# HGRN2 attention and a max-out FFN in one kernel: the first part reordered, and the block loads issued in odd units

## The chip, the cores and the metric

The kernel runs on one core of one Trainium2 chip. The metric is the device time of that core in microseconds (us). Three runs of the kernel before took 503.63, 503.81 and 504.72 us; their median is 503.81. Engines have their short names: PE is TensorE (matrix products), PEld its weight loads, DVE is VectorE, ACT is ScalarE, POOL is GpSimd, SP is the sync engine, whose queue issues most of the DMAs. "SPq" and "ACTq" in the profile are the issuing queues of SP and ACT.

## What is computed

Attention first, with B = 4 batches, H = 8 heads, S = 768 steps and D = 48; then an FFN over the 3072 tokens with model width 384 and hidden width 768. All is fp32.

```
f = 1 / (1 + exp(-f_logit))
for t in range(S):
    state = f[:, :, t, :, None] * state + einsum('bhd,bhe->bhde', k[:, :, t], v[:, :, t])
    y[:, :, t] = einsum('bhd,bhde->bhe', q[:, :, t], state)
x = y.transpose(0, 2, 1, 3).reshape(B * S, H * D)
h = maximum(maximum(x @ w1, x @ w2), x @ w3)
out = h @ w_out
```

The FFN weights arrive as 64-bit words and are rounded to fp32 on the chip.

## The kernel before, in words

**Units and groups.** The work of the attention is cut into 24 units (NU). Unit u is a chunk of 64 time steps (c = u // 2) of a pair of batches (u % 2), so 128 tokens. Four units (GRP) are one group of 512 tokens, and each of the six groups gets one FFN.

**Functions of a unit.** `load` (L161) fetches f, k and q: for units below 8 by rows, two DMAs a tensor (L158); from unit 8 on by blocks, for two units at once, as 24 DMAs (L173), called where u is even. `load_v` (L178) fetches v with two DMAs. `sigmoids` makes the gates, `after` a backward scan (L273) and kh (L280), `before` a forward scan (L287) and qh (L291), `carry` (L297) the decayed state, `keys` (L306) transposes kh and copies it to ks on ACT (L308), `pairs` (L319, L322) makes the masked products at, `values` (L333, L342) the outputs y and the new state (st, L350), `finish` (L363) adds what comes from the state and copies y to `heads` on ACT (three copies, L369). `pack` (L373) rearranges heads into xT, the FFN's input, by ten DMAs (L380). It is called as pack(0, 2) for three units of a group, on SP, and as pack(3, 3) for the last, five DMAs on SP and five on ACT in turn. In the first group it is one call for all four units, on both queues.

**FFN.** `ffn` (L385) is a generator. Its 18 steps are three products 128x512 each (L392; a product shows as two records of the profile), with the maximum kept on ACT (L396) and DVE (L398), into hm. Its four out groups are six products 128x384 each (L411), a copy to `o` on ACT (L414) and two DMAs to the output (L418). `fill(n)` (L423) runs n such pieces of the FFN at a place of the attention's code; so each engine's order is written out by hand in the schedule (L437 to L535), and the FFN of a group runs between the units of the next.

**Buffers.** The pool `work` has two buffers a name (o, top, xT), unless a number is given; hm has one. Of the PSUM tiles named p for the FFN there are two. The copy of out group i + 2 thus waits for the two output DMAs of group i, and the product after next waits for that copy.

**Weights.** There are 24 pieces: 18 of w1 to w3 and 6 of w_out. `load_weights` (L190) fetches raw words (L199), at most 12 pieces ahead. `round_begin` (L203) has two ACT instructions (L211, L216), two on DVE (L212, L213) and an add on POOL (L217); `round_end` (L220) one on DVE (L225) that writes w_in or w_out. Three pieces are rounded in the first part, the others inside ffn(0), one ahead. `pad_blocks` (L140) writes constants beside the block loads with six POOL memsets, after units 4 and 6.

**Queues.** The DMAs of SP are issued in the order of the code. In the built program each DMA issue of SP and ACT takes one of eight completion semaphores, which the two queues share, and an issue waits until the DMA before it on the same semaphore has landed.

**End.** After the last FFN, DVE, TensorE and DVE again (L538 to L543) compute `low`, which says whether a gate product fell below a limit; SP, TensorE and the others read it (L732) and branch (L733) to a general version, which does not run with these inputs.

The loop around the places that the change touches is this:

```
for u in range(GRP, NU):
    n = u + 1
    fill(2 if u % 2 and u > 2 * GRP else 1)
    keys(u)
    if u > GRP:
        finish(u - 1)
        if u % GRP == 3:
            pack(0, 2, xT)
        elif u % GRP == 0:
            pack(3, 3, xT, both)
```

Of the kernel before, what the change touches and what calls it, by code (L numbers as in the profile page):

```python
# [9 lines left out]
FP32 = mybir.dt.float32  # L10
I32 = mybir.dt.int32
U32 = mybir.dt.uint32
AF = mybir.ActivationFunctionType
ALU = mybir.AluOpType
# [40 lines left out]
def kernel(  # L55
# [32 lines left out]
    def fast():  # L88
        ctx = ExitStack()
        with ctx:  # L90
# [47 lines left out]
                    nc.vector.memset(t[:, :, D:DP], pad)  # L138

            def pad_blocks(i):  # L140
                for nm, pad in PADS.items():
                    for p0 in (32, 96):
                        nc.gpsimd.memset(blocks[nm][i][p0:p0 + 32, :, :, D - 32:], pad)

            NLD = 4
            BY_ROWS = 8
# [31 lines left out]
            def load_v(u):  # L178
                load_tokens(v_tiles[u % NLD], v, u)
# [20 lines left out]

            halfway = {}

            def round_begin(n):  # L203
                if n in raw:
                    words = raw[n].rearrange("p (c two) -> p c two", two=2)
                    lo, hi = words[:, :, 0], words[:, :, 1]

                    top = work.tile([128, PIECE], U32, name="top_bits", bufs=4)  # L210
                    nc.scalar.activation(top.bitcast(FP32), hi.bitcast(FP32), AF.Abs)  # L211
                    nc.vector.tensor_scalar(top.bitcast(FP32), top.bitcast(FP32), HI_MIN, None, op0=ALU.max)  # L212
                    nc.vector.tensor_scalar(top, top, 3, 0x3FFFFFF8, op0=ALU.logical_shift_left, op1=ALU.bitwise_and)  # L213

                    rest = work.tile([128, PIECE], U32, name="rest_bits", bufs=3)
                    nc.scalar.activation(rest, lo, AF.Copy, scale=2.0 ** -29)  # L216
                    nc.gpsimd.tensor_tensor(top, top, rest, op=ALU.add)  # L217
                    halfway[n] = (top, hi)

            def round_end(n):  # L220
                if n in raw:
                    top, hi = halfway.pop(n)
                    dst = pieces[n][0].bitcast(U32)
                    by = lambda t: t.rearrange("p (a c) -> p a c", a=dst.shape[1])
                    nc.vector.scalar_tensor_tensor(dst, by(hi), 0xC0000000, by(top),  # L225
                                                   op0=ALU.bitwise_and, op1=ALU.bitwise_or)
                    raw.pop(n)
# [157 lines left out]
            def ffn(g, xT):  # L385
                hm = work.tile([128, NJ, TOK], FP32, name="hm", bufs=1)
                for j in range(NJ):
                    top = None
                    for i in range(3):
                        p = ps_f.tile([128, TOK], FP32, name="p")  # L390
                        for kt in range(NK):
                            nc.tensor.matmul(p, lhsT=w_in[i][:, kt, j * 128:(j + 1) * 128], rhs=xT[:, kt, :],  # L392
                                             start=(kt == 0), stop=(kt == NK - 1))
                        if i == 0:
                            top = work.tile([128, TOK], FP32, name="top")
                            nc.scalar.copy(top, p)  # L396
                        else:
                            nc.vector.tensor_tensor(hm[:, j, :] if i == 2 else top, p, top, op=ALU.max)  # L398

                        if g == 0:  # L400
                            step, last = 3 * j + i, 3 * NJ
                            for r in range(*(3 + (len(pieces) - 3) * n // last for n in (step, step + 1))):
                                round_end(r)
                                if r + 1 < len(pieces):
                                    round_begin(r + 1)
                            load_weights(2, r + 1)
                        yield
                for i in range(GRP):
                    p = ps_f.tile([128, TOK], FP32, name="p")
                    for j in range(NJ):  # L410
                        nc.tensor.matmul(p[:, 0:DM], lhsT=hm[:, j, i * UT:(i + 1) * UT], rhs=w_out[:, j, :],  # L411
                                         start=(j == 0), stop=(j == NJ - 1))
                    o = work.tile([UT, DM], FP32, name="o")
                    nc.scalar.copy(o, p[:, 0:DM])  # L414
                    c, bp = divmod(g * GRP + i, 2)
                    for a in range(2):
                        t0 = (2 * bp + a) * S + c * C
                        nc.sync.dma_start(out=out[t0:t0 + C, :], in_=o[a * C:(a + 1) * C, :])  # L418
                    yield
# [3 lines left out]
            def fill(n):  # L423
                while n and pending:
                    try:
                        next(pending[0])
                        n -= 1
                    except StopIteration:
                        pending.pop(0)

            def new_xT():
                return work.tile([128, NK, TOK], FP32, name="xT")

# [3 lines left out]
            with tc.manual_schedule():  # L437
# [2 lines left out]
                load(1, one, "kq")  # L440
                load_v(0)
                load(2)
                load_v(1)
                load(3)
                load_weights(3)
                load_v(2)
                load_v(3)
                xT = new_xT()
                sigmoids(0)
# [8 lines left out]
                for u in range(2):  # L458
                    values(u)
                    keys(u + 1)  # L460
                    after(u + 2)
                    carry(u + 2)
                    pairs(u + 1)
                    finish(u)
                    before(u + 2)
                    if u == 0:
                        sigmoids(3)
                values(2)
                keys(3)
                finish(2)  # L470
                load_weights(3)
                load(GRP)
                load_v(GRP)
                round_begin(0)
                pairs(3)
                round_begin(1)
                round_begin(2)
                values(3)
                for n in range(3):
                    round_end(n)  # L480
                round_begin(3)

                nc.tensor.transpose(ps_tr.tile([128, 128], FP32, name="tr"), ident, ident)
                finish(3)
                pack(0, GRP - 1, xT, both)
                load_weights(3)
                load(GRP + 1)
                load_v(GRP + 1)
# [7 lines left out]
                fill(1)  # L496
                for u in range(GRP, NU):
                    n = u + 1
                    fill(2 if u % 2 and u > 2 * GRP else 1)
                    keys(u)  # L500
                    if u > GRP:
                        finish(u - 1)
# [4 lines that stand above are left out]
                    if u % GRP == 0:  # L507
                        if u > GRP:
                            pending.append(ffn(u // GRP - 1, xT))
                        xT = new_xT()  # L510
                    pairs(u)
                    if u + 2 < NU and (u % 2 == 0 or u + 2 < BY_ROWS):
                        load(u + 2)
                    if u + 2 < NU:
                        load_v(u + 2)
                    if n < NU:
                        sigmoids(n)
                    fill(1)
                    if n < NU:
                        after(n)  # L520
                    fill(1)
                    values(u)
                    if n < NU:
                        before(n)
                        carry(n)
                        if n in (5, 7):
                            pad_blocks(n // 2 % 2)
                    fill(1)
                    if u >= 2 * GRP:
                        fill(1)  # L530
                fill(1)
                finish(NU - 1)
                pack(3, 3, xT, both)
                pending.append(ffn(NU // GRP - 1, xT))
                fill(99)  # L535


            least = work.tile([128, 1], FP32, name="least")  # L538
            nc.vector.tensor_reduce(out=least, in_=ends.rearrange("p u a -> p (u a)"), op=ALU.min, axis=AX.X)
            nc.vector.tensor_scalar(least, least, P_MIN, None, op0=ALU.is_lt)  # L540
            n_low = ps_tr.tile([1, 1], FP32, name="tr")
            nc.tensor.matmul(n_low, lhsT=least, rhs=ones, start=True, stop=True)
            nc.vector.tensor_copy(low, n_low)  # L543

    def general():
        G, AHEAD = 128, 3
# [218 lines left out]
```

## Time and profile before

| | us |
|---|---|
| median of three runs | 503.81 |
| the profiled execution | 504.31 |
| its span in the trace | 502.6 |
| PE busy | 467.9 (93%) |
| DVE busy | 217.2 (43%) |
| ACT busy | 108.7 (22%) |
| POOL busy | 98.7 (20%) |
| L392 (FFN products), busy | 291.9 |
| L411 (out products), busy | 98.8 |

The mean granted TensorE clock is 0.966. The page cuts the span in 40 equal slices; a digit is the busy share of a slice in tenths, and 9 is 90% or more. The chain is the work that ended last, followed back from the last instruction to what released it. A row of a group gives the line, the engine, the tiles out<-in, the shape and the count, then the busy time, the mean ns of one instruction, and the idle time of the engine just before them with what ended most of it. A line of the waits gives the engine and line that waited, what it waited for, the us in total, the times and the longest. A line of the timeline gives the start and length in us, the engine and line, and in brackets the idle time ahead of it with its releaser.

### The profile page before, as it was taken

The numbers are of one execution on the slowest core, as the hardware profiler recorded it, in microseconds if no ns is written. First come the engines' busy times: TensorE is split into PE (matmuls) and PEld (weight loads), VectorE is DVE, ScalarE is ACT, GpSimd is POOL, SyncE is SP. The second block draws the span as 40 slices with busy tenths as digits, with TensorE's granted clock in tenths as the row PEclk, the third lists the DMA queues.
The fourth block names the chain that finished last, engine by engine and source line by source line (L and its number), as shares of the span: only waits on it lengthen the run. The fifth ranks groups of instructions, "written<-read, shape, count | busy, mean of one in ns | idle before, by whom it ended". The sixth has DMA issues, their size and how long they took to land.

```text
span 502.6 us, 9969 instructions
## 1 busy us (share of the span) xinstructions
PE 467.9 (93%) x4067; PEld 250.9 (50%) x4067; DVE 217.2 (43%) x346; ACT 108.7 (22%) x227; POOL 98.7 (20%) x132
## 2 busy tenths in 40 slices
PE   5755999996989999999999999999999999999994
PEld 4642555543635455645545654545644545544452
DVE  7852787787225435135535226533325620012100
ACT  2340445540212211202220211220220111100000
POOL 2111356564021212021112022112112200000000
PEclk9875999998999999999999999999999999999998
DMA  9995996720156612266602276402460011200011
GB/s 129 199 179 157 268 243 143 93 59 1 40 87 109 88 27 65 46 79 110 85 2 63 56 88 109 66 16 57 78 105 18 1 36 37 55 0 0 1 28 42
DMA packets 170007, 38.51 MB, mean 77 GB/s; under 512 B 154976, under 2 KB 168800, under 8 KB 169952
## 3 DMA queue, kind: packets, MB, share of 16 engines
q1 hardware_dynamic: 166208, 36.50, 41.5%
q10 hardware_dynamic: 3744, 1.28, 1.3%
q8 instruction: 34, 0.56, 0.5%
q14 instruction: 21, 0.17, 0.1%
HBM read 28.31 MB, written 4.72 MB: 66 GB/s over the span
## 4 chain that ended last, share of the span: by engine, by line
PE 80%; DVE 6%; DMA 4%; SPq 4%; ACT 1%; issue 1%; POOL 1%; ACTq 0%; DVEq 0%; POOLq 0%
PE p L392 53%; PE p L411 17%; SPq L158 3%; PE y L363 2%; PE y L333 2%; DMA xT<-heads 2%; PE a L319 2%; PE tr L306 2%; PE y L342 1%; DMA v_ld<-in_v_dram 1%; POOL top_bits L217 1%; PE tr L234 1%; DVE top_bits L213 1%; DMA k_ld<-in_k_dram 1%; DVE top_bits L212 1%
## 5 line engine op out<-in xcount | busy, mean ns | idle before, releaser
L392 PE MATMUL p<-xT,w_in 128*128 128x512 f32 x648 | 291.9, 602 | 7.3 <-DMA xT<-heads 5.1
L392 PEld LDWEIGHTS p<-xT,w_in 128*128 128x128 f32 x648 | 120.5, 191 | 147.0 <-issue 134.1
L411 PE MATMUL p<-w_out,hm 128*128 128x384 f32 x288 | 98.8, 501 | 4.3 <-DVE w_out L225 4.3
L411 PEld LDWEIGHTS p<-w_out,hm 128*128 128x128 f32 x288 | 55.5, 195 | 44.7 <-DVE w_out L225 5.6
L398 DVE TENSOR_TENSOR top<-p,top 128x512 f32<-128x512 f32 x36 | 24.8, 690 | 106.3 <-PE p L392 106.3
L396 ACT COPY top<-p 128x512 f32<-128x512 f32 x36 | 21.1, 586 | 191.5 <-PE p L392 191.5
L279 POOL COPY ends<-r 128x8 f32<-128x8 f32 x24 | 4.6, 193 | 194.2 <-DVE r L273 194.2
L398 DVE TENSOR_TENSOR hm<-p,top 128x512 f32<-128x512 f32 x36 | 24.6, 684 | 38.2 <-PE p L392 38.2
L322 DVE TENSOR_TENSOR at<-a,mask 128x512 f32<-128x512 f32 x24 | 16.5, 689 | 52.8 <-PE a L319 52.8
L217 POOL TENSOR_TENSOR top_bits<-top_bits,rest_bits 128x384 uint32<-128x384 uint32 x24 | 27.2, 1133 | 50.3 <-DVE top_bits L213 27.9
L414 ACT COPY o<-p 128x384 f32<-128x384 f32 x24 | 11.4, 477 | 107.8 <-PE p L411 99.0
L287 DVE TENSOR_TENSOR_SCAN prod<-gate,from_inv 128x520 f32<-128x520 f32 x24 | 32.4, 1349 | 0.0
L273 DVE TENSOR_TENSOR_SCAN r<-gate,from_one 128x520 f32<-128x520 f32 x24 | 30.9, 1288 | 2.9 <-issue 2.2
L369 ACT COPY heads<-y 64x256 f32<-64x256 f32 (+1 forms) x72 | 26.6, 369 | 14.3 <-PE y L363 13.3
L291 POOL TENSOR_TENSOR qh<-qt,prod 128x512 f32<-128x512 f32 x16 | 18.8, 1178 | 41.7 <-DVE qt L238 41.7
L333 PEld LDWEIGHTS y<-at,v_ld 64*64 64x64 f32 x768 | 13.9, 136 | 20.9 <-issue 16.7
L333 PE MATMUL y<-at,v_ld 64*64 64x64 f32 x768 | 17.3, 227 | 5.7 <-ACT rest_bits L216 2.7
L308 ACT COPY ks<-tr 128x512 f32<-128x512 f32 x22 | 12.9, 586 | 41.2 <-PE tr L306 40.9
L280 POOL TENSOR_TENSOR kh<-kt,r 128x512 f32<-128x512 f32 x16 | 19.0, 1186 | 14.2 <-DVE kt L238 14.2
L297 POOL TENSOR_TENSOR state<-st,ends 128x384 f32<-128x384 f32 x22 | 21.1, 958 | 0.2
L238 DVE STREAM_TRANSPOSE gate<-sig 128x512 f32<-128x512 f32 x16 | 11.3, 708 | 21.2 <-ACT sig L254 21.2
L319 PE MATMUL a<-qh,kh 48*64 48x64 f32 x768 | 16.5, 225 | 0.5 <-DVE qh L291 0.5
(64 smaller groups left out, 269.9 us busy)
## 6 DMA issues: line engine op xcount, KB each, us to landing
raw<-in_moe_w_dram SPq DMA_DIRECT2D x18, 384.0 KB, 5.1
v_ld<-in_v_dram SPq DMA_DIRECT2D x48, 96.0 KB, 3.3
out_dram<-o SPq DMA_DIRECT2D x48, 96.0 KB, 2.2
raw<-in_moe_w_out_dram SPq DMA_DIRECT2D x6, 384.0 KB, 4.1
xT<-heads SPq DMA_DIRECT2D x30, 72.0 KB, 2.1
f_ld<-in_f_logit_dram SPq DMA_DIRECT2D x32, 64.0 KB, 2.9
k_ld<-in_k_dram SPq DMA_DIRECT2D x32, 64.0 KB, 2.8
q_ld<-in_q_dram SPq DMA_DIRECT2D x32, 64.0 KB, 2.8
```

The costliest lines, as they stand in the source:

```text
L217: nc.gpsimd.tensor_tensor(top, top, rest, op=ALU.add)
L273: nc.vector.tensor_tensor_scan(r[:, 0:LEN][:, ::-1], flat(gate)[:, ::-1], flat(from_one)[:, ::-1], 1.0, op0=ALU.mult, op1=ALU.max)
L280: (nc.vector if u < BY_ROWS else nc.gpsimd).tensor_tensor(kh.rearrange("p h a t -> p a h t"), kt, by_batch(r[:, 1:LEN + 1].rearrange("p (x ...
L287: nc.vector.tensor_tensor_scan(flat(prod), flat(gate_tiles[u % 2]), flat(from_inv[u % 2]), 1.0, op0=ALU.mult, op1=ALU.max)
L297: nc.gpsimd.tensor_tensor(t, states[u % 2], ends[:, u, :].unsqueeze(2).to_broadcast([128, 2 * HP, D]), op=ALU.mult)
L319: nc.tensor.matmul(p[t, par, hp * C:(hp + 1) * C], lhsT=kh[r, hp, a, :], rhs=qh[r, a, hp, :], start=True, stop=True)
L333: nc.tensor.matmul(y[o:o + DP, a, hp * C:(hp + 1) * C], lhsT=v_ld[s, 2 * hp + par, :], rhs=d["at"][s, par, hp, :], start=(hp == 0), stop=F ...
L369: nc.scalar.copy(heads[o, :, t0 + a * C:t0 + (a + 1) * C], y[i, a, 0:HP * C].rearrange("p (h t) -> p h t", h=HP))
L392: nc.tensor.matmul(p, lhsT=w_in[i][:, kt, j * 128:(j + 1) * 128], rhs=xT[:, kt, :], start=(kt == 0), stop=(kt == NK - 1))
L396: nc.scalar.copy(top, p)
L398: nc.vector.tensor_tensor(hm[:, j, :] if i == 2 else top, p, top, op=ALU.max)
L411: nc.tensor.matmul(p[:, 0:DM], lhsT=hm[:, j, i * UT:(i + 1) * UT], rhs=w_out[:, j, :], start=(j == 0), stop=(j == NJ - 1))
```

## The change

1. The order of the first part. The loads of f for unit 3 stand before the v loads of units 1 and 2, and v of unit 2 before the raw words. `round_begin` is split: its two ACT instructions stay, DVE's and POOL's become `round_middle`, and rest_bits has four buffers instead of three. Pieces 0 and 1 are begun before values(2), piece 2 after pairs(3), pieces 3 and 4 after the packing; round_end(0) stands before finish(3), 1 and 2 after it. Inside ffn(0) rounding runs two pieces ahead instead of one. Before the packing only f and k of unit 4 are loaded; its q and v are loaded after it.
2. `busy(n)`: n products 128x256 of constants, whose result is not used; three times one in the first part, and 14 while x of the first group is packed.
3. The six memsets of `pad_blocks` are given out one by one, at the steps and out groups of ffn(0).
4. The block loads are issued in odd units, three units ahead (unit 7 loads for 10 and 11, unit 9 for 12 and 13), instead of in even ones, two ahead.
5. At unit 8 no piece of the FFN runs before keys(8), so from there on only one out group instead of two stands before a group's last finish.
6. The computation of `low` stands after the first eight pieces taken from the end of the last unit on, inside the last FFN, instead of after it.

```diff
@@ pad_blocks
-                        nc.gpsimd.memset(blocks[nm][i][p0:p0 + 32, :, :, D - 32:], pad)
+                        yield nc.gpsimd.memset(blocks[nm][i][p0:p0 + 32, :, :, D - 32:], pad)
@@ round_begin
+                    lo, hi = words(n)
                     top = work.tile([128, PIECE], U32, name="top_bits", bufs=4)
                     nc.scalar.activation(top.bitcast(FP32), hi.bitcast(FP32), AF.Abs)
+
+                    rest = work.tile([128, PIECE], U32, name="rest_bits", bufs=4)
+                    nc.scalar.activation(rest, lo, AF.Copy, scale=2.0 ** -29)
+                    halfway[n] = (top, rest)
+
+            def round_middle(n):
+                if n in raw:
+                    top, rest = halfway[n]
                     nc.vector.tensor_scalar(top.bitcast(FP32), top.bitcast(FP32), HI_MIN, None, op0=ALU.max)
                     nc.vector.tensor_scalar(top, top, 3, 0x3FFFFFF8, op0=ALU.logical_shift_left, op1=ALU.bitwise_and)
-                    rest = work.tile([128, PIECE], U32, name="rest_bits", bufs=3)
-                    nc.scalar.activation(rest, lo, AF.Copy, scale=2.0 ** -29)
                     nc.gpsimd.tensor_tensor(top, top, rest, op=ALU.add)
@@ ffn
                                 round_end(r)
-                                if r + 1 < len(pieces):
-                                    round_begin(r + 1)
+                                if r + 2 < len(pieces):
+                                    round_begin(r + 2)
+                                    round_middle(r + 2)
                             load_weights(2, r + 1)
+                            next(pads, None)
...
+                    if g == 0:
+                        next(pads, None)
@@ new
+            def busy(n):
+                p = ps_f.tile([128, TOK], FP32, name="p")
+                for _ in range(n):
+                    nc.tensor.matmul(p[:, 0:256], lhsT=ident, rhs=from_one.rearrange("p x t -> p (x t)")[:, 0:256],
+                                     start=True, stop=True)
+
+            pads = iter(())
@@ schedule
                 load(2)
+                load(3, one, "f")
                 load_v(1)
-                load(3)
+                load(3, one, "kq")
+                load_v(2)
                 load_weights(3)
-                load_v(2)
...
                     pairs(u + 1)
+                    busy(1)
                     finish(u)
...
+                for n in range(2):
+                    round_begin(n)
                 values(2)
+                for n in range(2):
+                    round_middle(n)
                 keys(3)
                 finish(2)
                 load_weights(3)
-                load(GRP)
-                load_v(GRP)
-                round_begin(0)
+                load(GRP, one, "fk")
                 pairs(3)
-                round_begin(1)
+                busy(1)
                 round_begin(2)
+                round_middle(2)
                 values(3)
-                for n in range(3):
-                    round_end(n)
-                round_begin(3)
+                round_end(0)
...
                 finish(3)
+                round_end(1)
+                round_end(2)
                 pack(0, GRP - 1, xT, both)
+                for n in range(3, 5):
+                    round_begin(n)
+                    round_middle(n)
+                busy(14)
+                load(GRP, one, "q")
+                load_v(GRP)
                 load_weights(3)
@@ loop over units
-                    fill(2 if u % 2 and u > 2 * GRP else 1)
+                    fill(0 if u == 2 * GRP else 2 if u % 2 and u > 2 * GRP else 1)
...
-                    if u + 2 < NU and (u % 2 == 0 or u + 2 < BY_ROWS):
+                    if u + 2 <= BY_ROWS:
                         load(u + 2)
+                    elif u % 2 and u + 3 < NU:
+                        load(u + 3)
...
-                            pad_blocks(n // 2 % 2)
+                            pads = pad_blocks(n // 2 % 2)
@@ end
                 pending.append(ffn(NU // GRP - 1, xT))
+                fill(8)
+                least = ...
+                n_low = ps_tr.tile([1, 1], FP32, name="tr")
+                nc.tensor.matmul(n_low, lhsT=least, rhs=ones, start=True, stop=True)
+                nc.vector.tensor_copy(low, n_low)
                 fill(99)
```

More of the change, by code (lines that the diff above doesn't have):

```diff
@@ L201, in fast, with words @@
             halfway = {}
+            def words(n):
+                w = raw[n].rearrange("p (c two) -> p c two", two=2)
+                return w[:, :, 0], w[:, :, 1]
             def round_begin(n):
                 if n in raw:
-                    words = raw[n].rearrange("p (c two) -> p c two", two=2)
-                    lo, hi = words[:, :, 0], words[:, :, 1]
+                    lo, hi = words(n)
                     top = work.tile([128, PIECE], U32, name="top_bits", bufs=4)
                     nc.scalar.activation(top.bitcast(FP32), hi.bitcast(FP32), AF.Abs)
+                    rest = work.tile([128, PIECE], U32, name="rest_bits", bufs=4)
[4 more added lines that the diff above has]
+                    top, rest = halfway[n]
                     nc.vector.tensor_scalar(top.bitcast(FP32), top.bitcast(FP32), HI_MIN, None, op0=ALU.max)
                     nc.vector.tensor_scalar(top, top, 3, 0x3FFFFFF8, op0=ALU.logical_shift_left, op1=ALU.bitwise_and)
-                    rest = work.tile([128, PIECE], U32, name="rest_bits", bufs=3)
-                    nc.scalar.activation(rest, lo, AF.Copy, scale=2.0 ** -29)
                     nc.gpsimd.tensor_tensor(top, top, rest, op=ALU.add)
-                    halfway[n] = (top, hi)
             def round_end(n):
                 if n in raw:
-                    top, hi = halfway.pop(n)
+                    (top, _), (_, hi) = halfway.pop(n), words(n)
                     dst = pieces[n][0].bitcast(U32)
@@ L534, in fast @@
                 pending.append(ffn(NU // GRP - 1, xT))
-                fill(99)
[L538 to L543, printed above, removed]
+                fill(8)
+                least = work.tile([128, 1], FP32, name="least")
+                nc.vector.tensor_reduce(out=least, in_=ends.rearrange("p u a -> p (u a)"), op=ALU.min, axis=AX.X)
+                nc.vector.tensor_scalar(least, least, P_MIN, None, op0=ALU.is_lt)
+                n_low = ps_tr.tile([1, 1], FP32, name="tr")
+                nc.tensor.matmul(n_low, lhsT=least, rhs=ones, start=True, stop=True)
+                nc.vector.tensor_copy(low, n_low)
+                fill(99)
     def general():
```

## The prediction

> **What bounds the kernel now.** I read the page first (busy shares, slices, chain), then the waits of TensorE and of the SP queue, then the timeline round each idle place of TensorE.
>
> ```profile
> PE 467.9 (93%) x4067; PEld 250.9 (50%) x4067; DVE 217.2 (43%) x346; ACT 108.7 (22%) x227; POOL 98.7 (20%) x132
> PE   5755999996989999999999999999999999999994
> PEclk9875999998999999999999999999999999999998
> PE 80%; DVE 6%; DMA 4%; SPq 4%; ACT 1%; issue 1%; POOL 1%; ACTq 0%; DVEq 0%; POOLq 0%
> L392 PE MATMUL p<-xT,w_in 128*128 128x512 f32 x648 | 291.9, 602 | 7.3 <-DMA xT<-heads 5.1
> ```
>
> TensorE bounds it: busy 93%, 80% of the chain, and at 9 in every slice of 12.6 us except the first four, the tenth (113 to 126), the twelfth (138 to 151) and the last. So work added on TensorE counts one for one, another engine's work counts only where TensorE comes to wait for it, and a gain can only come from the slices that are not full.
>
> ```profile
> PE tr L234 <- DMA f_ld<-in_f_logit_dram: 8.4, 4, 4.7
> PE p L392 <- DMA xT<-heads: 5.1, 2, 4.1
> PE p L411 <- DVE w_out L225: 4.3, 2, 2.9
> PE y L333 <- ACT rest_bits L216: 2.7, 1, 2.7
> PE y L333 <- DMA v_ld<-in_v_dram: 2.3, 1, 2.3
> PE p L392 <- ACT o L414: 2.2, 1, 2.2
> ```
>
> Columns: total us, times, longest. These are what the change aims at. Loading f costs 8.4, packing x 5.1, rounding of w_out 4.3, rounding ahead of the values 2.7, v 2.3, the o copy 2.2. Now the SP queue:
>
> ```profile
> SPq L418 <- ACT o L414: 89.0, 14, 49.1
> SPq L380 <- ACT heads L369: 82.8, 8, 31.6
> SPq L380 <- DMA xT<-heads: 24.4, 3, 21.7
> ```
>
> The third line is the one to understand. Its 21.7 us lie here:
>
> ```profile
> 107.20 27.89 SPq L380 DMA_DIRECT2D xT<-heads  x10
> 131.52 3.21 ACTq L380 DMA_DIRECT2D xT<-heads  x5
> 136.68 2.50 SPq L418 DMA_DIRECT2D out_dram<-o  x4
> 139.28 3.10 SPq L380 DMA_DIRECT2D xT<-heads  x5
> 141.95 2.60 PE L392 MATMUL p<-xT,w_in 128*128 128x512 f32 x5 [2.18 <-ACT o L414]
> ```
>
> SP issued seven of the ten DMAs of pack(0, 2) by 111.6 and the eighth at 133.30, when ACT's first DMA of pack(3, 3), issued at 131.52, had landed (133.28). In the built program every DMA issue of SP and ACT takes one of eight completion semaphores in turn, and waits until the DMA before it on the same one has landed; here that was ACT's, which needs heads of unit 7. So SP stood still until unit 7 was finished. It cost little, since behind it lay two v loads, four outs and five xT DMAs.
>
> **What the Trainium skill says.** "DMA: Bandwidth & Descriptors", section "Anatomy of one DMA — SWDGE (gpsimd) path": DMA engines don't wait on semaphores, any wait happens on the issuing sequencer before dispatch. The trace agrees: a blocked issue holds all that SP has behind it (21.7 us). The same page, "Issuing engines are not separate DMA queues": using two issuing engines saves only issue time; the trace has 0.6 us an issue on either. "TensorE: Matmul & The Clock Gate", "Part 1: The HAM clock gate": after an idle window of about 3.4 us the clock halves, and one busy window restores it. The trace agrees: the granted clock changes in steps of 3.41 us, 0.5 in 35.40 to 52.46 and 120.73 to 127.56, and 1.0 from there to 499.6.
>
> **Part 1, the first part.** Two terms of the wait list go: 2.3 for v (v2 now ahead of the raw pieces) and 2.7 for rounding in front of values(3) (ACT's rounding no longer stands between at and heads). The f load of unit 3, which now stands ahead of its v loads, takes a further share of the 8.4. The three busy(1) lie in stretches where TensorE waits anyway. In before ACT copies heads of unit 3 at 39.22 to 40.36. In after the eight ACT instructions of 0.54 us that ran at 33.07 to 36.7 are largely elsewhere and v and f come sooner: I put these copies at 32.6 to 33.8. What is late next is the packing: the loads of f4 and k4 still stand ahead of it on SP (q4 and v4 go behind it, and are needed only by before(4) and values(4), after step 2), and the rows' DMAs share a bandwidth in which half a row tile lands each 0.65 us. I estimate the last xT landing at 40.3 (39.5 to 42), against 46.62. While x is packed, busy(14) keeps TensorE at work: a 128x512 matmul is 0.86 us warm and 1.72 cold, so a 128x256 one is 0.43 to 0.86 by estimate, 14 take 6 to 12 us, and end near 40: beside the packing, not after it. If they end later, up to 42.2, they delay step 0. With the clock up, the three matmuls of step 0 take 2.58 us and end near 42.6 (41 to 45), against 50.09; before also ran cold to 52.46, another 1.2. **Gain 8.7.**
>
> **Part 2, rounding two pieces ahead, pads one at a time.** From 111.9 to 121.5 the out group waits 4.75 us for w_out (DVE L225), and the clock is 0.5 from 120.73 to 127.56, which costs 3.05 more. With rounding begun a piece earlier and POOL's six memsets of 3.87 us in one piece no longer between, most of it goes; I leave 0.75 (0 to 2.5). **Gain 7.0.** If DVE or POOL has no slack there, it is the next wait.
>
> Sum to unit 7: before takes 129.62 − 50.09 = 79.53 us from step 0's end to finish(7). Less 1.2, 4.75 and 3.05, and less one out group of 3.87 that fill(0) moves behind it, 66.7 are left; with 0.75 finish(7) starts at 42.6 + 66.7 + 0.75 = **F = 110.1** (107.5 to 113).
>
> **Part 3, block loads in odd units.** Behind finish TensorE has: pairs to F + 1.06, two out groups to F + 9.0 (206.84 to 214.85 in group 2 of before, F = 205.78), values to F + 10.07, the last out group (six matmuls, 3.87) to F + 13.95; there the next FFN wants xT. In the order of the changed program SP has, in unit 7: pack(0, 2), the 24 block loads of unit 10, two v, out(0), and only then its five DMAs of pack(3, 3). The semaphores fall so that the **first** DMA of pack(0, 2) now waits for ACT's first of pack(3, 3), where it was the eighth. So SP is blocked to F + 3.66 (133.28 − 129.62), and then issues ten xT at 0.61 (to F + 9.8), 24 loads at 0.55 to 0.58 (8 took 4.88 at the least loaded place; to F + 23.6), two v at 0.7, two outs at 0.6 (to F + 26.3) and five xT, which land 1.78 after issue: first third F + 28.7, last F + 30.6. Step 0 starts there instead of F + 13.95. Then the out copies: work tiles named o have two buffers, the copy of i = 3 waits for the outs of i = 1, which stand behind xT and v, landing F + 33.7. So step 1 starts at F + 34.25 instead of F + 16.53: **17.7 lost** (16 to 20), and 1.7 for a cold window after it (0 to 3.4).
>
> Groups 2, 3 and 4 (units 11, 15, 19): here pack(0, 2) and 14 loads get out before the blocked issue; at F + 3.9 (209.68 in before) ten loads, two v, out(0) and five xT follow: xT lands F + 14.2 to 16.1, just late, the outs of i = 1 at F + 19.1, step 1 starts at F + 19.7 instead of 16.5: 3.2 each. Idle this long mostly halves the next window (0.7 times 1.7 = 1.2). **4.4 each, 13.2 in all** (0.5 to 6.5 each). Group 5 has no loads any more: nothing.
>
> **Part 4, least and n_low in the last FFN.** In before the reduce ran at 394.9, hidden. Now TensorE meets n_low right behind a max on DVE: 0.69 + 0.31 + 0.15 us of DVE work, 1.3 lost (0.5 to 2). At the end the load of low no longer follows the last out on SP (issued 496.23, landed 500.10; load 496.88 to 497.61, branch 498.0), but that landing binds next: **gain 0.6** (0 to 1.2).
>
> **Sum.** Before, step 0 of the second FFN starts at 141.95 and TensorE is full from there to 495.14. After, the like point is F + 13.95 + 17.7 + 1.7 = 143.5, so 1.5 later; then + 13.2 + 1.3 − 0.6 = +15.4. The profiled execution took 504.31 (span 502.6 and 1.7 round it), which gives 519.7; the median shown is 0.5 lower: **519**.
>
> **Rivals.**
> A. SP's block does not decide, because xT arrives in time. For it: TensorE has 14 us behind finish, and SP in before used up 12.3 of them without much harm. Against: 24 loads are 13.4 us of issue alone. Then gains of 8.7 + 7.0 + 2.2 (the o wait) + 0.6 stand against 1.3: 503.8 − 17.2 = 486.6; with one group late by a few us up to 500. The other side; it decides once those five xT DMAs are issued by F + 12. Chance 0.12.
> B. Only the group of unit 7 stalls; in groups 2 to 4 the queues drain quicker (o copies early enough). Then 519 − 13.2 = 505.8, and with F at its early end 503.2. For it: xT misses by only 0.3 to 2 us there. Against: out(1) is behind xT on SP. 0.16: of it 0.05 within 0.2% and 0.01 below.
> C. The front gives less: half rows and raw pieces share the DMA engines, and rounding two ahead competes with scans for DVE, F = 113 to 116. Then 522 to 525. 0.17.
> D. Each stall also costs two cold windows and the first part gives less: above 526. 0.05.
> The forecast (509 to 522): 0.50.
>
> **How the numbers follow.** The range reaches from B's 504 to C's 526, which leaves out A and D, some 0.17 to 0.2. By sign, with 0.2% (1 us) as about what a measurement of this kernel can tell from no change: faster 0.13, same 0.05, slower 0.82.
>
> **What would show it.** Right: finish of unit 7 near 110; SP's ten L380 issues of that unit as one stretch that ends only after ACT's five; TensorE idle some 14 us behind it, put down to the xT DMA, and 2 to 3 us in each of three later groups, put down to o or xT; PEclk below 9 at each; the waits for w_out and rest_bits gone. Wrong: no idle stretch of TensorE after unit 7, or finish of unit 7 later than 113.

## The result, and the profile after

The changed kernel took 521.0 us (median of four runs, 516.18 to 522.49), the kernel before 503.79 on the same terms: a ratio of 1.0321, 95% interval 1.0251 to 1.0391. The prediction was 519.0. The profiled execution of after is the fastest of the four, 516.18 us with a span of 514.4, so the sums below are made against 516.18 − 504.31 = 11.9. Line numbers of after are ten to fifteen higher: L401 is the FFN product (L392 before), L422 the out product (L411), L389 the xT DMA (L380), L427 the o copy (L414).

The page of after, the lines that answer to those of before:

```profile
PE 472.2 (92%) x4101; PEld 252.1 (49%) x4101; DVE 223.4 (43%) x346; ACT 108.9 (21%) x227; POOL 99.4 (19%) x132
PE   5889999986499999799999889999989999989995
PEclk9999999989599999999999989999999999999999
PE 82%; SPq 8%; DMA 5%; DVE 2%; issue 1%; ACT 0%; POOL 0%; ACTq 0%; DVEq 0%; POOLq 0%
L401 PE MATMUL p<-xT,w_in 128*128 128x512 f32 x648 | 294.2, 605 | 22.5 <-DMA xT<-heads 14.2
```

The second to the fourth slice are fuller than before and the first four have the full clock: that is the gain of the first part. The new hole is in the tenth and eleventh slice (6 and 4, the clock at 5), and shallow ones follow. On the chain SPq has gone from 4 to 8%, and the idle time ahead of the FFN products from 7.3 to 22.5 us. The waits of TensorE in after (us in total, times, longest):

```profile
PE p L401 <- DMA xT<-heads: 14.2, 4, 11.2
PE p L401 <- ACT o L427: 7.8, 4, 3.2
PE tr L243 <- DMA f_ld<-in_f_logit_dram: 6.4, 3, 4.7
PE y L342 <- DMA v_ld<-in_v_dram: 1.5, 3, 1.1
PE a L328 <- POOL qh L300: 1.4, 1, 1.4
...
PE tr L577 <- DVE least L575: 1.3, 1, 1.3
...
PE p L422 <- DVE w_out L234: 0.6, 1, 0.6
```

Most of what the change aimed at became smaller: w_out 4.3 to 0.6, rest_bits 2.7 to nothing, f 8.4 to 6.4, v 2.3 to 1.5. The other two grew: xT from 5.1 to 14.2 and the o copy from 2.2 to 7.8, 22.0 us together, and there are two small new ones (qh, least). The waits of the SP queue:

```profile
SPq L389 <- DMA xT<-heads: 14.3, 2, 13.6
...
SPq L174 <- DMA xT<-heads: 10.9, 3, 4.2
```

The first is the block at unit 7, the second the block inside the block loads of three later groups (L174 is a block load). The queues in after behind the finish of unit 7, which TensorE starts at F = 106.98 (the first line is ACT's, the others are SP's):

```profile
108.88 3.30 ACTq L389 DMA_DIRECT2D xT<-heads  x5
110.68 6.29 SPq L389 DMA_DIRECT2D xT<-heads  x10
117.07 4.29 SPq L174 DMA_DIRECT2D f_ld<-in_f_logit_dram  x8
121.41 4.76 SPq L174 DMA_DIRECT2D k_ld<-in_k_dram  x8
126.21 4.20 SPq L174 DMA_DIRECT2D q_ld<-in_q_dram  x8
130.46 1.37 SPq L159 DMA_DIRECT2D v_ld<-in_v_dram  x2
131.93 1.22 SPq L431 DMA_DIRECT2D out_dram<-o  x2
133.24 3.10 SPq L389 DMA_DIRECT2D xT<-heads  x5
```

And TensorE, which had finished the last out group at 124.5:

```profile
135.72 5.18 PE L401 MATMUL p<-xT,w_in 128*128 128x512 f32 x6 [11.20 <-DMA xT<-heads]
141.37 5.42 PE L401 MATMUL p<-xT,w_in 128*128 128x512 f32 x12 [0.47 <-ACT o L427]
```

The ten xT DMAs of pack(0, 2), which could have gone when unit 6 was finished, started only at F + 3.70, when ACT's first DMA, issued at 108.88, had landed (110.62); 24 loads, two v and two outs followed, and the five DMAs that the FFN waited for came last. The three later group ends:

```profile
219.69 5.42 PE L401 MATMUL p<-xT,w_in 128*128 128x512 f32 x12 [2.40 <-ACT o L427]
297.59 7.05 PE L401 MATMUL p<-xT,w_in 128*128 128x512 f32 x12 [3.17 <-ACT o L427]
377.11 5.42 PE L401 MATMUL p<-xT,w_in 128*128 128x512 f32 x12 [1.77 <-ACT o L427]
```

Up to step 1 of the second FFN after is ahead (141.37 against 144.53, 3.2 us). From there to the last product before takes 350.6 us without idle time, after 366.7: 12.0 idle (10.5 in three group ends, 1.3 for least, 0.2 else) and 4.1 of slower products. Of these, 1.6 are a cold window, which is 3.41 us at half the clock: the twelve records at 297.59 took 7.05 instead of 5.42. Most of the rest is in products beside the idle places (the six records of step 0 took 3.16 us at 214.13 and at 291.27, against 2.74 where TensorE came without a pause). The end behind the last product is 1.1 shorter. − 3.2 + 16.1 − 1.1 = 11.8, the difference of the spans. The other three runs had a mean granted clock of 0.966 to 0.972 against 0.978 in the profiled one; by estimate, 0.008 of 514 us is 4.1 us more lost to the clock, about what they took longer (3.9 to 6.3). Where they lost it no trace shows. Which idle place is followed by a cold window isn't settled by its length alone: in after one of the three later group ends has one, in e3 (below) all three, with idle times of 2.4 to 2.8 us for the o copy.

### The profile page after: what moved, and what is told of

The parts are those of the page before. It is cut to its first block, busy times and chain, and to the rows that moved or that the text cites. A ratio compares the mean times of both kernels' runs of the same rounds, so it can differ in the third digit from the quotient of the medians.

```text
span 514.4 us, 10046 instructions
## 1 busy us (share of the span) xinstructions
PE 472.2 (92%) x4101; PEld 252.1 (49%) x4101; DVE 223.4 (43%) x346; ACT 108.9 (21%) x227; POOL 99.4 (19%) x132
## 4 chain that ended last, share of the span: by engine, by line
PE 82%; SPq 8%; DMA 5%; DVE 2%; issue 1%; ACT 0%; POOL 0%; ACTq 0%; DVEq 0%; POOLq 0%
PE p L401 54%; PE p L422 16%; SPq L159 4%; PE y L342 3%; PE y L372 2%; PE a L328 2%; DMA out_dram<-o 2%; PE y L351 2%; PE tr L315 1%; DMA v_ld<-in_v_dram 1%; SPq L431 1%; PE p L448 1%; PE tr L243 1%; SPq L174 1%; SPq L389 1%
## 5 line engine op out<-in xcount | busy, mean ns | idle before, releaser
L401 PE MATMUL p<-xT,w_in 128*128 128x512 f32 x648 | 294.2, 605 | 22.5 <-DMA xT<-heads 14.2
L401 PEld LDWEIGHTS p<-xT,w_in 128*128 128x128 f32 x648 | 120.7, 192 | 166.2 <-issue 132.6
L422 PE MATMUL p<-w_out,hm 128*128 128x384 f32 x288 | 98.3, 497 | 0.6 <-DVE w_out L234 0.6
L422 PEld LDWEIGHTS p<-w_out,hm 128*128 128x128 f32 x288 | 54.8, 193 | 38.9 <-issue 3.9
L427 ACT COPY o<-p 128x384 f32<-128x384 f32 x24 | 11.4, 476 | 142.5 <-PE p L422 74.5
L227 POOL TENSOR_TENSOR top_bits<-top_bits,rest_bits 128x384 uint32<-128x384 uint32 x24 | 28.2, 1175 | 36.9 <-DVE top_bits L225 25.1
L296 DVE TENSOR_TENSOR_SCAN prod<-gate,from_inv 128x520 f32<-128x520 f32 x24 | 34.8, 1451 | 0.0
L300 POOL TENSOR_TENSOR qh<-qt,prod 128x512 f32<-128x512 f32 x16 | 18.8, 1176 | 39.5 <-DVE qt L247 39.5
L317 ACT COPY ks<-tr 128x512 f32<-128x512 f32 x22 | 12.8, 582 | 41.9 <-PE tr L315 41.9
L306 POOL TENSOR_TENSOR state<-st,ends 128x384 f32<-128x384 f32 x22 | 20.3, 924 | 0.2
```

The source lines that it names most:

```text
L296: nc.vector.tensor_tensor_scan(flat(prod), flat(gate_tiles[u % 2]), flat(from_inv[u % 2]), 1.0, op0=ALU.mult, op1=ALU.max)
L306: nc.gpsimd.tensor_tensor(t, states[u % 2], ends[:, u, :].unsqueeze(2).to_broadcast([128, 2 * HP, D]), op=ALU.mult)
```

## The experiments

The theory is that of the prediction: SP's queue is the wait, because a DMA issue must wait for one of ACT's on the same completion semaphore, and because 24 block loads stand between the two halves of the packing. The rivals: the loads by themselves are too many; only their order counts; the front's gain is lost somewhere else. Times are medians, in brackets the ratio to before and its 95% interval; "before" ran beside each set (503.6 to 504.0).

**e3: pack(3, 3) on SP alone.**

```diff
                         elif u % GRP == 0:
-                            pack(3, 3, xT, both)
+                            pack(3, 3, xT)
```

> The changed kernel with pack(3, 3) of units 8, 12, 16 and 20 issued by SP alone (ten DMAs) instead of by SP and ACT in turn; block loads stay in odd units. Theory (SP's queue is blocked because DMAs of SP and ACT share completion semaphores): with no ACT DMA there, pack(0, 2) and the block loads get out before unit 7 is finished at 107, xT lands at about F + 10, the stalls of all four groups go, and the time is that of the kernel before less 21 (front 18.8, o wait 2.2), plus 1.3, less 0.8: 483 to 486 us. Rival (24 loads in the odd unit are too many for the queue or the DMA engines by themselves): five more DMAs on SP behind the same loads, so xT is later still, 521 to 526 us.

Measured: 513.53 us (1.0215, 1.0171 to 1.026). The expectation failed, by 27.5 us above the top of its range, and its rival (521 to 526) too. Pack(0, 2) did start at once (96.98), and step 1 came at F + 25.1 instead of F + 34.4, so without the block, and with five more DMAs on SP, the stall is 9.3 shorter. But SP then is busy without a pause: pack(0, 2), loads, v and outs to 119.9, and ten xT to 127.2. From the finish of unit 6 to that of unit 7 it is only 12.8 us (94.64 to 107.45), and the DMAs from 96.98 to 119.9 take 23. In the later groups the stalls stayed, 2.4 to 2.8 us each for the o copy and up to 0.6 for xT:

```profile
211.53 7.11 PE L401 MATMUL p<-xT,w_in 128*128 128x512 f32 x12 [2.45 <-ACT o L427]
290.44 7.11 PE L401 MATMUL p<-xT,w_in 128*128 128x512 f32 x12 [2.44 <-ACT o L427]
369.49 7.11 PE L401 MATMUL p<-xT,w_in 128*128 128x512 f32 x12 [2.77 <-ACT o L427]
```

So the block is half of the matter at unit 7, and not what decides later on.

**e8 and e1: block loads in even units again**, once with the piece of the FFN ahead of keys(8) as before (e8), once without it (e1).

```diff
-                    if u + 2 <= BY_ROWS:
-                        load(u + 2)
-                    elif u % 2 and u + 3 < NU:
-                        load(u + 3)
+                    if u + 2 < NU and (u % 2 == 0 or u + 2 < BY_ROWS):
+                        load(u + 2)
...
-                    fill(0 if u == 2 * GRP else 2 if u % 2 and u > 2 * GRP else 1)
+                    fill(2 if u % 2 and u > 2 * GRP else 1)
```

The second part of this diff is in e8 alone.

> The changed kernel with parts 4 and 5 undone: block loads in even units and an FFN piece before keys(8), as before; the first part, rounding, busy and the early low stay. Theory: this is what the front is worth, with the smaller stall of the kernel before at unit 8 (xT at about F + 14.2 against F + 12.3): 486 to 490 us. Rival (the front's gain is only borrowed and lost again at a later place): 498 to 504 us.

> The changed kernel with part 4 alone undone (block loads in even units), while no FFN piece runs before keys(8), so out group 1 comes after the loads in SP's order. Theory (what decides is where SP's outs and xT stand in the queue): the group of unit 7 stalls as long as in the changed kernel, now for the o copy, whose outs are behind 24 loads (F + 34), and the later groups stall about 8 us each instead of 4: 531 to 537 us. Rival (block loads in odd units are what costs): 484 to 490 us.

Measured: e8 493.91 (0.9814, 0.9786 to 0.9843), e1 535.57 (1.0618, 1.0581 to 1.0655). The wait of TensorE ahead of the FFN products, in e8 and in e1:

```profile
PE p L401 <- DMA xT<-heads: 6.0, 1, 6.0
```

```profile
PE p L401 <- ACT o L427: 36.6, 4, 15.3
```

In e8 all later stalls are gone, and the gain of the first part reaches the end; my number was 4 to 8 us too low, because TensorE still waits 6.0 for xT at unit 7 (there the fourth DMA of pack(0, 2) is blocked, to 115.6). e1 came as its theory had it and answers the rival that odd units as such are bad: with even ones, and out group 1 left behind the loads in SP's order, TensorE waits 15.3, 6.5, 7.8 and 7.0 us for the o copy. Where the FFN piece is moved, odd units are the better place for the loads (521.0 against 535.6); what counts is what stands behind 24 loads. The fourth combination, odd units with the FFN piece kept ahead of keys(8), was not run, so what part 4 costs by itself isn't shown.

**e13 and e14: block loads of units 7, 11, 15 and 19 ahead of pack(0, 2)**, with pack(3, 3) on SP alone (e13) or as in after (e14).

```diff
                         if u % GRP == 3:
+                            if u + 3 < NU:
+                                load(u + 3)
                             pack(0, 2, xT)
...
-                    elif u % 2 and u + 3 < NU:
+                    elif u % GRP == 1 and u + 3 < NU:
                         load(u + 3)
```

> e3 (pack(3, 3) on SP alone), with the block loads of units 7, 11, 15 and 19 put ahead of pack(0, 2) instead of behind it. Theory, amended: at unit 7 SP is short of time (24 loads of unit 6, ten xT, 24 loads and 14 more DMAs in a row, each some 0.6 us), so order changes little there, 1 us; in the later groups SP stood idle before pack(0, 2), so loads ahead of it are out in time and the stalls of 2.8 to 3.1 us with their cold windows go, 4.4 each: 498 to 501 us. Rival (the stalls of the later groups come from the out and xT transfers themselves, not from loads ahead of them in the queue): as e3, 512 to 515 us.

> The changed kernel with only the block loads of units 7, 11, 15 and 19 put ahead of pack(0, 2); pack(3, 3) stays on SP and ACT. Theory: in the group of unit 7 the first load now waits for ACT's first xT DMA, with all else behind it, so that stall stays at 17 to 18 us; in the later groups the blocked issue is an xT DMA with no load behind it, and their stalls go: 506 to 510 us. Rival (order of loads and pack decides in the group of unit 7 too): below 500 us.

Measured: e13 493.25 (0.979, 0.9762 to 0.9818), e14 505.32 (1.0039, 1.0018 to 1.0061), just under its theory's 506. With after and e3 they make a square:

| us | loads behind pack(0, 2) | loads ahead of it |
|---|---|---|
| pack(3, 3) on SP and ACT | 521.0 | 505.3 |
| pack(3, 3) on SP alone | 513.5 | 493.3 |

The order is worth 15.7 and 20.3, the queue 7.5 and 12.1. In e14 the stall at unit 7 is as long as in after (step 1 at F + 35.1), and in three later groups 0.9 us of idle time is left of 10.5. So by the medians the later groups hold 15.7 of what after lost, 5.2 each, clock included. From step 1 to the end the traces of after and e14 differ by 12.9 us, 4.3 a group, and those of e3 and e13 by 16.0, 5.3 a group. A line of e14's SP queue, in the third group, shows what makes a block all but harmless, and the line of TensorE what is left of the stall there:

```profile
185.04 22.11 SPq L389 DMA_DIRECT2D xT<-heads  x10
```

```profile
218.37 5.42 PE L401 MATMUL p<-xT,w_in 128*128 128x512 f32 x12 [0.91 <-ACT o L427]
```

SP stood there for most of 22 us behind a blocked xT DMA, as in before, but the loads were already out, and no more than these 0.9 us came of it; the two groups after it have no idle place. In e13 no later group stalls; step 1 at unit 7 comes at F + 23.4, since SP is still out of time there. e13 came out 5 us under its range. Much of that goes with the clock: 0.988 to 0.991 in its runs against 0.965 to 0.974 in e3's, and e3's trace has a cold window at each of the three later group ends, e13's none.

**e7: e8 with pack(3, 3) on SP alone**, and **e18: the same on the kernel before.** The edit is that of e3.

> e8 (block loads in even units, an FFN piece before keys(8)) with pack(3, 3) on SP alone. Theory: the 6.0 us that TensorE waits for xT after unit 7 in e8 come from the shared semaphores too (SP stood from 97 to 115.6); without ACT's DMAs they go, with the cold windows that follow (3.4), and the time is 484 to 487 us. Rival (ten DMAs on SP take 3.1 us longer than five, so xT is late by as much): 492 to 496 us.

> The kernel before with pack(3, 3) of units 8, 12, 16 and 20 issued by SP alone, nothing else. Theory: in before the blocked SP queue cost only the wait for the o copy at unit 8 (2.2 us), since few DMAs stood behind it: 501 to 502.5 us. Rival (SP alone for pack(3, 3) is a gain of some 8 us of its own, which e7 shows over e8): 495 to 497 us.

Measured: e7 486.08 (0.9646, 0.9614 to 0.9679), e18 502.14 (0.9964, 0.9949 to 0.9979). Both as the theory had it. In e7 TensorE goes from the values of unit 8 to the FFN without a pause (124.66); in e18 the 2.2 us for the o copy are gone (step 0 at 140.22 against 141.95, with F half a us later), and the other stalls of before are all there. The difference of e7 and e18, 16.1 us, is what the first part, the rounding and the early low are worth together.

**e5 and e15: without busy(14)**, taken from e3 and from e7.

```diff
-                busy(14)
```

> e3 (pack(3, 3) on SP alone) without busy(14), the 14 products of constants during the packing. Theory: TensorE idles 6 us there, the clock is granted at half for one or two windows of 3.41 us, and the time is 2 to 4 us above e3. Rival (the products only fill an idle place): the same as e3 within 0.5 us.

> e7 without busy(14). If the products keep the clock up: 2 to 4 us above e7. If they only fill an idle place: the same as e7 within 0.5 us. From e5 against e3 (0.9 us, less than the spread of the runs) I put more on something between, 1 to 3 us.

Measured: e5 514.39 (e3: 513.53), e15 486.68 (0.9661, 0.9621 to 0.9701; e7: 486.08). Neither difference stands out of the spread of the runs, and both lie under what was expected (2 to 4, and 1 to 3). The timelines of e7 and e15 show why. TensorE in e7, with the products (L448; two records each):

```profile
34.64 8.24 PE L448 MATMUL p<-from_one,ident 128*128 128x256 f32 x28
42.72 2.74 PE L401 MATMUL p<-xT,w_in 128*128 128x512 f32 x6
45.29 0.60 PE L243 MATMUL tr<-ident,f_ld 128*128 128x128 f32 x4
```

and in e15, without them:

```profile
38.76 2.04 PE L401 MATMUL p<-xT,w_in 128*128 128x512 f32 x2 [4.03 <-DMA xT<-heads]
41.81 3.73 PE L401 MATMUL p<-xT,w_in 128*128 128x512 f32 x4 [1.01 <-DMA xT<-heads]
45.36 0.62 PE L243 MATMUL tr<-ident,f_ld 128*128 128x128 f32 x4
```

With the products the granted clock is at half to 38.59, without them to 45.39. But they take 8.24 us, partly cold themselves, and end after the last xT landed (42.07). Without them step 0 starts 4 us earlier at half speed. Both reach the next instruction at 45.3. In these traces the products paid for themselves and no more; a smaller number is tried below.

**e16: rounding one piece ahead**, and **e17: low after the last FFN**, both from e7.

```diff
-                                if r + 2 < len(pieces):
-                                    round_begin(r + 2)
-                                    round_middle(r + 2)
+                                if r + 1 < len(pieces):
+                                    round_begin(r + 1)
+                                    round_middle(r + 1)
...
-                for n in range(3, 5):
+                for n in range(3, 4):
```

> e7 with rounding one piece ahead instead of two in ffn(0) (and piece 4 begun there and not in the first part); the memsets of the pads stay one by one. Theory as predicted (rounding ahead is what removed the wait for w_out): the wait of 4.3 us and some of its cold clock come back, 489 to 494 us. Rival (POOL's six memsets in one piece were what made w_out late, and giving them out one by one is enough): 486 to 487 us.

> e7 with the computation of low back after the last FFN (part 6 undone). By the step as predicted (1.3 us of TensorE waiting for the reduce against 0.6 us at the end): 0.7 us faster than e7, about 485.4. From the trace of the changed kernel (the end shorter by 1.1 us): 0.2 us faster. Rival (the early load of low is worth the whole chain at the end, 2 us or more): 2 us slower.

Measured: e16 489.09 (0.9699, 0.9676 to 0.9723), e17 486.10 (0.9638, 0.9604 to 0.9671). In e16 this wait of TensorE is back at half of its old size:

```profile
PE p L422 <- DVE w_out L234: 2.1, 2, 1.5
```

From the end of step 0 to the finish of unit 7 e16 takes 67.7 us, against 65.3 in e7 (one out group, which stands in between in both, left out), so rounding two ahead with piece 4 begun early is worth 2.4. The other half of the 4.3 stays away without it. The memsets given out one by one can be what took it, but round_begin is split and the first pieces are rounded earlier in e16 too, and no run parts these. The clock stays up in e16, so the second half of part 2's loss doesn't return. e17 can't be told from e7: the wait of 1.2 for least is gone, the end is longer by about as much.

**e19: e7 with busy(8), and the reduce of least ahead of the last finish.**

> e7 with busy(8) instead of busy(14), and the reduce of least moved ahead of the last finish, so that n_low does not wait for it. Theory: 1.2 us from n_low, and up to 2 us from the products, which in e7 ended 1 us after the last xT had landed: 483 to 485 us. Rival (without the longer cover the clock falls and takes the gain back): 486 us.

Measured: 484.32 us (0.961, 0.9588 to 0.9632), the fastest of all; its interval overlaps that of e7, so the step from e7 is likely, not shown. Its trace has neither the wait for least nor more than 1.0 us of idle time ahead of the FFN products, and what follows step 0 starts at 43.3 instead of 45.3. That this is due to the fewer products isn't shown either: five traces with busy(14) have step 0 done as soon or sooner (after 41.7, e3 42.2, e8 42.7, e14 43.2, e13 43.4).

## Why the prediction was right, point by point

- **The front** (parts 1 and 2). Heads of unit 3 were copied from 32.66 (predicted 32.6), the last xT landed at 39.87 (40.3), step 0 ended at 41.7 (42.6), F was 106.98 (110.1). Without the out group that moved behind it, before had 125.75, so the front gained 18.8 instead of 15.6. The step that was mis-sized is the work between step 0 and finish: 66.7 + 0.75 was put there, 65.3 was taken. These 65.3 are the same in all eight traces of this front (after, e1, e3, e7, e8, e13, e14, e17; an out group that stands ahead of the finish left out), while the end of step 0 goes from 41.7 (after) to 45.5 (e7), and F with it from 107.0 to 110.7. So 18.8 is the best of eight, 15.0 the least. Two readings were off without weight: 0.41 of the 4.75 us put to w_out is another wait (4.3 in the line shown), and POOL's six memsets took 3.6 us (105.67 to 109.26), not 3.87.
- **The block at unit 7.** First xT at F + 3.70 (predicted F + 3.66), the last five issued at F + 26.3 (F + 26.3), step 0 at F + 28.74 (F + 28.7), step 1 at F + 34.39 (F + 34.25). This was read from the kernel's own semaphores and the rates of before, and the queue kept to it; so did the first 14 loads ahead of the block in the third group. What TensorE did in between moved: its last out group ended at F + 17.5 instead of F + 13.95 (the wait for qh below and a cold window), so it idled 11.2 us and not some 14. The clock then was at half to 140.48, step 0 took 5.18 us instead of 2.58, and 0.47 was left to wait for the o copy. So the cold window that was put behind step 1, 1.7 us, was hidden in step 0 and wasn't paid. e3 and e13 add what the prediction did not say: even without the block SP has too little time there, and about half of the stall remains.
- **The later groups.** Idle time 3.75, 3.35 and 3.43 us, 10.5 in all; predicted 3.2 each, and 4.4 with the clock. In the trace of after the idle time and the slower products make 14.6, 4.9 each, with a cold window in one group of three; by e14 against after it is 4.3 each in the traces and 5.2 by the medians. The prediction gave the block as the reason that xT and outs were late; e3 takes the block away and the stalls stay at 2.4 us and more for the o copy. There e3's five more xT DMAs on SP (3.1 us) take the place of the block of 4.2, so it does not clear the block wholly; e14 shows that the block alone, with the loads out early, costs 0.9 us in all. So there it is the loads' place that decides, and how much the block adds to it is open: the prediction had the late outs and xT right, but only a part of their reason.
- **Part 5 was costed at nothing**, and that step failed, though it was hidden. The FFN piece ahead of keys(8) had covered DVE's scan and POOL's qh of unit 8. Without it TensorE waits 1.4 us for qh (after, e1, e3, e5, e13, e14; not e7, e8), and in after and e3 a cold window follows (24 records of the out products took 9.70 instead of 8.01), in e1, e5, e13 and e14 none. In after xT comes later still, so it cost nothing there.
- **Part 6**: 1.3 for least (predicted 1.3), 1.1 at the end (0.6): next to nothing in all, as e17 has it.
- **busy(14)**: I had it beside the packing and ending near 40; in after it ended at 38.8. I let it carry the clock, 1.2 us and the speed of step 0. In after the products ran at full clock and step 0 was done at 41.7, sooner than in the traces without them (e5 42.9, e15 45.5). In e7 they ran half cold, and it was 45.5. In the medians the gain is no larger than what the products delay.
- **The sum** is closer than its terms. The profiled execution took 11.9 us more than that of before, where 15.4 was forecast: the front was 3.1 better, the cold window at unit 7 not paid, the end 0.5 better, the later groups 1.4 worse, and the rest is small. That the median came so near to 519 is partly luck: the other three runs took 3.9 to 6.3 us longer at a lower clock, which the sum doesn't hold. Rival A (no stall, 486.6) is close to what e7 shows to be the worth of the other parts: 486.1.

What stays open: how many cold windows the other runs of after had, and where; whether two ahead or the early piece 4 made the difference in e16; and what the changed kernel takes with part 5 alone undone.

## What to carry to other kernels

Read what stands in an issuing queue behind each instruction that can block, and add up the issue times between the moment its input is ready and the moment its output is needed: a block is nearly free while only late work stands behind it (1.5 us on the kernel before, by e18), and costs the bound engine when bulk loads do. Moving bulk transfers earlier in the order can put them in front of the small ones that the bound engine waits for. Where queues share completion semaphores, see on which DMA of the other queue each issue waits: keeping one tensor's DMAs on one queue was worth 7.8 us in e7 against e8, and some 1.5 on the kernel before.

## What the runs showed of the hardware

SP took 0.53 to 0.60 us for the issue of a block load and 0.61 to 0.63 for an xT DMA (8 in 4.20 to 4.76, 10 in 6.29), so 24 block loads are 13 us of its queue, while the DMA engines were busy to 59, 71 and 75% in the three stretches of eight loads behind the block in after. Each load landed some 2 to 4 us after its issue, and the next was issued without waiting for it.

The granted clock was 1.0 or 0.5, in stretches of 3.41 us or whole multiples of it. The same wait of 1.4 us for qh was followed by such a stretch at half clock in after and e3, and by none in e1, e5, e13 and e14. e3 and after, with idle places at the later group ends, varied by 6 us from run to run (510.2 to 516.4, 516.2 to 522.5), e13 without them by 2. But the idle places alone don't make the spread: e1, with idle places of 6.5 to 15.3 us, varied by 3, and e5 by 2.
